# Linear attention followed by a mixture of adapters: the order of the second half rewritten, with the division moved to GpSimd for slots 18 to 35

## The chip, the cores and the metric

The kernel runs on one core of one Trainium2 chip. The core has TensorE (PE in the profile), VectorE (DVE), ScalarE (ACT), GpSimd (POOL) and SyncE (SP), which run side by side and wait for each other by semaphores; each takes its own instructions strictly in the order in which they were written. The metric is the device time of one execution in microseconds (us), and lower is better. A measurement of this kernel tells about 0.5% from no change.

## The reference

```
phi(x) = concat(relu(x) * cos(theta), relu(x) * sin(theta))      theta = pi/2 * position / S
kv  = sum over s of phi(k)[s,f] * v[s,d]      z = sum over s of phi(k)[s,f]
num = phi(q) @ kv                             den = phi(q) . z + 1e-6
x   = (num / den), heads side by side         q, k, v: 8 batches x 8 heads x 576 positions x 64
logits = x @ w_gate (8 experts); the two largest take part, weighted by their softmax
out = x + sum over the two experts e of weight_e * (x @ A[e]) @ B[e]          rank 16, float32 out
```

x has 4608 rows (batch and position) of 512 values.

## The kernel before

**Batches and slots.** Each of the 8 batches has a first part: q, k and v are loaded (float32 in memory, bfloat16 in the core's SBUF), v is multiplied by the cosine and by the sine of the position (`vs`: 9 position groups s, two tables i, so 18 instructions of 256 elements for each batch), k goes through relu (`rk`), and 72 small matmuls in three parts (`kv`) form the sums, which ACT copies to SBUF (`kve`). The 4608 rows of x are worked in 36 slots of 128 rows. Nine slots make two batches; the fifth of nine (4, 13, 22, 31) holds 64 rows of each of the two batches and is called mixed.

**The steps of a slot n.** `qc` relu of q, twice for a batch; `qt` four transposes on PE; `qe` DVE multiplies them by the tables into qT; `nd` PE forms numerators and denominators in one PSUM tile `nd` of 128 x 520 float32, of which there is only one; `re` DVE takes the reciprocals of the 8 denominators; `no` DVE multiplies the 512 numerators by them into x in bfloat16 (lines 354 to 363); `xt` PE transposes x; `xe` ACT copies that to SBUF; `za` PE forms gate logits and adapter products; for each group of three slots DVE finds the two largest logits and the weights (`mx`, `nm`, `mk`, `tt`, `cb`, `zg`, with a sigmoid `sg` on ACT), PE transposes (`zt`), and the result is copied (`ze`). `dx` is two matmuls of 512 columns that add x and the adapters' part in PSUM, `oe` copies the output row block to SBUF, `st` stores its 256 KB.

**nd in two forms.** Usually `nd` contracts 128 rows at once, with blocks of zeros in kv: 8 matmuls of 130 columns (line 343), 16 for a mixed slot. `by_rows(n)` chooses a form in which the two halves of the rows work side by side on 65 columns each, without the zeros: 16 matmuls at line 332. Before, that holds for slots from 27 on that aren't mixed.

**The order.** The text `ORDER` gives every step with its engine and arguments (`no,V,18` is step `no` of slot 18 on DVE; A is ACT, T PE, S SP, G GpSimd). Each engine's queue is the part of the text that names it, in that order; waits between engines follow from the data and the buffers. `W` is GpSimd too, with one wait more (lines 512 to 518): the instruction waits until the last `vs`, `rk` or `qc` of DVE ahead of it in the text is done. Loads are issued by GpSimd (line 215), stores by SP. `gate` (line 236) holds the stores back until the last v has arrived. The first 358 steps, up to `qc,V,4,1`, stay as they are.

Of the kernel before, what the change touches and what calls it, by code (L numbers as in the profile page):

```python
# [21 lines left out]
ldv,S,0,0 pre,G start,A ldk,S,0,0 ldw,S ldq,G,0,0 tq,A ldv,G,1,0 ldk,G,1,0 ldq,G,1,0 ldv,G,2,0 vs,A,0,3,0  # L22
vs,V,0,5,1 ldk,G,2,0 cols,V vs,A,0,4,1 vs,V,0,7,1 vs,A,0,5,0 kz,G,1 kz,V,2 vs,A,0,8,0 vs,A,0,8,1 vs,A,0,1,0
vs,V,0,4,0 vs,A,0,7,0 kz,V,0 vs,A,0,0,1 vs,A,0,2,1 vs,A,0,0,0 vs,V,0,6,0 vs,A,0,1,1 vs,A,0,3,1 rk,V,0,0 rk,A,0,1
vs,V,0,2,0 vs,V,0,6,1 kv,T,0,0 qc,V,0,1 kv,T,0,1 qc,V,0,0 kv,T,0,2 qt,T,1 kve,A,0,0 qt,T,0 kve,A,0,1 qe,V,0
cw,A,0 qe,V,1 dm,T,n0 dm,T,n0 dm,T,n0 nd,T,0 qt,T,3 re,V,0 qt,T,2 no,V,0 qe,V,3 vs,G,1,8,0 vs,A,1,3,1 dm,T,b0
dm,T,b0 nd,T,1 vs,A,1,5,0 vs,G,1,6,1 vs,V,1,2,0 xt,T,0 vs,A,1,6,0 vs,W,1,7,1 xe,A,0 re,V,1 qe,V,2 vs,G,1,5,1
vs,A,1,8,1 vs,G,1,0,1 no,V,1 vs,A,1,2,1 ldq,G,2,0 vs,A,1,4,1 vs,V,1,1,1 dm,T,b0 dm,T,b0 dm,T,b0 dm,T,b0 dm,T,b0
dm,T,b0 nd,T,2 vs,V,1,1,0 vs,A,1,0,0 rk,V,1,0 ldv,G,3,0 xt,T,1 vs,A,1,7,0 xe,A,1 vs,V,1,4,0 ldk,G,3,0 dm,T,b0
kv,T,1,0 vs,V,1,3,0 re,V,2 za,T,0 no,V,2 ldq,G,3,0 kv,T,1,1 mx,V,0 nd,T,3 qc,V,1,0 xt,T,2 kv,T,1,2 re,V,3  # L30
qc,V,1,1 xe,A,2 za,T,1 no,V,3 kve,A,1,1 qt,T,4 qt,T,5 kve,A,1,0 za,T,2 qe,V,4 xt,T,3 mx,V,1 xe,A,3 mx,V,2 nd,T,4
# [48 lines left out]
oe,A,28 zg,V,10 xt,T,34 nd,T,35 oe,A,27 st,S,26 xe,V,34 za,T,33 oe,A,29 re,V,35 zt,T,10 no,V,35 za,T,34 ze,A,10  # L80
st,S,29 mx,V,33 mx,V,34 xt,T,35 nm,V,11 st,S,28 dx,T,31,q1 mk,V,11 tt,V,11 dx,T,30,q0 cb,V,11 st,S,27 xe,V,35
sg,A,11 dx,T,32,b0 oe,A,31 zg,V,11 oe,V,30 za,T,35 oe,A,32 zt,T,11 st,S,31 mx,V,35 ze,A,11 mk,V,12 nm,V,12
zm,V,12 st,S,32 dx,T,33,b1 sg,A,12 dx,T,34,q1 zg,V,12 st,S,30 oe,A,33 zt,T,12 oe,V,34 ze,A,12 st,S,33 dx,T,35,q0
st,S,34 oe,A,35 st,S,35
# [20 lines left out]
def by_rows(n):  # L105

    return n >= ROWS and not mixed(n)


@with_exitstack  # L110
def kernel(ctx, tc, q, k, v, w_gate, A, Bw, out):
# [432 lines left out]
```

## Time and profile before

| what | value |
|---|---|
| median of 3 runs | 106.09 us (105.9 to 106.48) |
| profiled execution: its own time | 105.77 us |
| profiled execution: span of its instructions | 104.0 us |
| PE busy / weight loads | 91.5 us (88%) / 65.8 us (63%) |
| DVE busy | 86.7 us (83%), 264 instructions |
| ACT busy | 81.3 us (78%), 176 instructions |
| POOL busy | 57.6 us (55%), 112 instructions |

The span goes from the first to the last instruction; the profiled execution's own time is 1.8 us longer, and 0.3 us below the median. Busy time is what an engine spent in instructions; neighbouring instructions overlap by a few hundredths of a us, so that the distance from start to start is the better price of one. In the page's 40 slices, DVE and PE are in the highest tenth nearly throughout from the eleventh to the thirty-fourth; POOL is at zero from the thirtieth on.

### The profile page before, as it was taken

The numbers are of one execution on the slowest core, as the hardware profiler recorded it, in microseconds if no ns is written. First come the engines' busy times: TensorE is split into PE (matmuls) and PEld (weight loads), VectorE is DVE, ScalarE is ACT, GpSimd is POOL, SyncE is SP. The second block draws the span as 40 slices with busy tenths as digits, with TensorE's granted clock in tenths as the row PEclk, the third lists the DMA queues.
The fourth block names the chain that finished last, engine by engine and source line by source line (L and its number), as shares of the span: only waits on it lengthen the run. The fifth ranks groups of instructions, "written<-read, shape, count | busy, mean of one in ns | idle before, by whom it ended". The sixth has DMA issues, their size and how long they took to land.

```text
span 104.0 us, 3983 instructions
## 1 busy us (share of the span) xinstructions
PE 91.5 (88%) x1620; PEld 65.8 (63%) x1620; DVE 86.7 (83%) x264; ACT 81.3 (78%) x176; POOL 57.6 (55%) x112
## 2 busy tenths in 40 slices
PE   4999899779794999999999999999989899998710
PEld 1334467467573887867887788787778576665200
DVE  5058769579995999999999999999999899999700
ACT  6969757918898689999799969989975895966720
POOL 6991004960799696997979869999910000000000
PEclk9999999999999999999999999999999999999997
DMA  2999999999999999999999999999999985699993
GB/s 27 369 353 292 215 210 247 207 209 211 205 207 210 208 208 208 207 215 202 207 210 207 214 202 207 209 207 129 198 404 395 382 308 220 251 381 385 384 381 143
DMA packets 19225, 25.55 MB, mean 246 GB/s; under 512 B 2184, under 2 KB 13448, under 8 KB 19208
## 3 DMA queue, kind: packets, MB, share of 16 engines
q0 software_dynamic: 11616, 12.98, 73.8%
q1 hardware_dynamic: 7064, 12.21, 32.7%
q8 instruction: 12, 0.20, 0.7%
q10 hardware_dynamic: 528, 0.13, 0.6%
q14 instruction: 5, 0.04, 0.1%
HBM read 28.85 MB, written 9.44 MB: 368 GB/s over the span
## 4 chain that ended last, share of the span: by engine, by line
PE 40%; DMA 20%; DVE 12%; ACT 10%; POOL 9%; issue 2%; POOLq 0%; SPq 0%; ACTq 0%
DMA q<-in_q_dram 18%; PE nd L343 8%; PE big L275 6%; PE xz L368 5%; PE za L377 4%; PE out L459 4%; PE pq L308 4%; PE out L458 4%; POOL vs L259 4%; DVE xt L362 4%; DVE qT L316 3%; DMA out_dram<-v0f 3%; ACT kvsb L294 2%; DVE qq L301 2%; ACT vs L258 2%
## 5 line engine op out<-in xcount | busy, mean ns | idle before, releaser
L259 POOL TENSOR_SCALAR vs<-v,tab 128x256 bf16<-128x256 bf16 x78 | 38.2, 506 | 17.2 <-DMA v<-in_v_dram 8.7
L372 ACT COPY xT<-xz 128x512 bf16<-128x512 bf16 x34 | 19.9, 587 | 9.6 <-PE xz L368 9.2
L316 DVE TENSOR_TENSOR qT<-pq,tabq 128x1024 bf16<-128x1024 bf16 x36 | 23.9, 677 | 0.8 <-PE pq L308 0.8
L258 ACT ACTIVATE vs<-v,tab 128x256 bf16<-128x256 bf16 x43 | 20.1, 511 | 1.0 <-DMA v<-in_v_dram 0.7
L343 PE MATMUL nd<-kvsb,qT 128*128 128x130 bf16 (+1 forms) x256 | 19.1, 222 | 0.4 <-DVE qT L316 0.4
L362 DVE TENSOR_TENSOR xt<-nd,rden 128x512 bf16<-128x512 f32 x28 | 19.2, 686 | 0.3
L275 PE MATMUL big<-vs,k 64*64 64x130 bf16 x576 | 12.4, 221 | 3.5 <-DVE k L266 1.7
L343 PEld LDWEIGHTS <-qT 128*128 128x128 bf16 (+1 forms) x256 | 13.6, 100 | 2.9 <-issue 1.2
L368 PE MATMUL xz<-ident,xt 128*128 128x128 bf16 x144 | 14.1, 220 | 1.0 <-DVE xt L362 0.7
L377 PE MATMUL za<-AW,xT 128*128 128x136 bf16 x144 | 14.4, 223 | 0.0
L275 PEld LDWEIGHTS <-k 64*64 64x64 bf16 x576 | 9.1, 106 | 6.3 <-DVE k L266 2.5
L308 PE MATMUL pq<-ident,qq 128*128 128x128 bf16 x144 | 13.0, 219 | 0.0
L459 PE MATMUL out<-Ball,zgT 128*128 128x512 bf16 x31 | 11.8, 379 | 0.4 <-ACT zgT L440 0.4
L487 PE MATMUL nd<-ones 128*128 128x512 bf16 x36 | 10.6, 469 | 1.5 <-DVE eps_hi L488 1.5
L458 PE MATMUL out<-xt,turn 128*128 128x512 bf16 x31 | 11.7, 379 | 0.1
L368 PEld LDWEIGHTS <-xt 128*128 128x128 bf16 x144 | 10.1, 114 | 2.3 <-DVE xt L362 0.9
L294 ACT CAST kvsb<-big 64x520 bf16<-64x520 f32 x16 | 9.5, 595 | 1.5 <-PE big L275 1.3
L377 PEld LDWEIGHTS <-xT 128*128 128x128 bf16 x144 | 9.4, 98 | 1.9 <-ACT xT L372 0.8
L308 PEld LDWEIGHTS <-qq 128*128 128x128 bf16 x144 | 9.2, 98 | 1.8 <-DVE qq L301 0.2
L338 PE MATMUL nd<-eps_hi,ones 128*128 128x4 bf16 x56 | 9.5, 170 | 0.1
L487 PEld LDWEIGHTS <-ones 128*128 128x128 bf16 x36 | 4.1, 116 | 7.5 <-issue 3.6
L301 DVE TENSOR_SCALAR qq<-q 128x1152 bf16<-128x1152 bf16 x16 | 7.8, 491 | 0.8 <-DMA q<-in_q_dram 0.8
(81 smaller groups left out, 146.4 us busy)
## 6 DMA issues: line engine op xcount, KB each, us to landing
q<-in_q_dram POOLq DMA_DIRECT2D x8, 576.0 KB, 17.2
v<-in_v_dram POOLq DMA_DIRECT2D x7, 576.0 KB, 17.7
k<-in_k_dram POOLq DMA_DIRECT2D x7, 576.0 KB, 16.9
out_dram<-k SPq DMA_DIRECT2D x10, 256.0 KB, 3.6
out_dram<-v0f SPq DMA_DIRECT2D x8, 256.0 KB, 4.2
out_dram<-k0f SPq DMA_DIRECT2D x8, 256.0 KB, 3.3
out_dram<-v SPq DMA_DIRECT2D x6, 256.0 KB, 2.9
v0f<-in_v_dram SPq DMA_DIRECT2D x1, 1152.0 KB, 5.6
```

Of the source, the lines that this page charges most:

```text
L258: return e.activation(dst, src, AF.Copy, bias=0.0, scale=t)
L259: return e.tensor_scalar(out=dst, in0=src, scalar1=t, scalar2=1.0, op0=ALU.mult, op1=ALU.mult)
L275: e.matmul(out=big[halves[g2], par, gp * 2 * W:(gp + 1) * 2 * W], lhsT=k_b[b][pr, 2 * gp + g2, s, :], rhs=vs_t[b % NV][pr, s, 2 * gp + g2, ...
L308: e.transpose(out=d[:, gp, :, jj, :], in_=q2_t[b % 3][:, gp, s].rearrange("p g d -> p (g d)"), identity=ident)
L316: e.tensor_tensor(out=qT_t[n % NQ], in0=src, in1=tab, op=ALU.mult)
L343: e.matmul(out=nd[pr, par, gp * 2 * W:(gp + 1) * 2 * W], lhsT=qT[:, i, gp * 2 + par, js], rhs=kv_t[b % 3][:, par, gp, i, :], start=False, ...
L362: e.tensor_tensor(out=x.rearrange("p (a t d) -> p t a d", t=2, d=D), in0=nds()[:, :, :, 0:D], in1=rd.rearrange("p (t a) -> p t a", t=2).to ...
L368: e.transpose(out=xz[:, c * 128:(c + 1) * 128], in_=x[:, c], identity=ident)
L372: (e.copy if e is nc.scalar else e.tensor_copy)(xT_t[n % 3], src)
L377: e.matmul(out=zs[:, i, :], lhsT=xT_t[n % 3][:, c, :], rhs=AW[:, c, :], start=(c == 0 and i == 0), stop=(c == DCH - 1), skip_group_check=True)
L458: e.matmul(out=d, lhsT=turn, rhs=x_t[n % NX], start=True, stop=False)
L459: e.matmul(out=d, lhsT=zgT_t[g % 3][:, n - GROUPS[g][0], :], rhs=Ball, start=False, stop=True)
```

## The change

From the 359th step on the text of the order is a new one. In it, for slots 18 to 35 (`SPLIT`), ACT copies the 520 sums of `nd` to SBUF as float32 (`ev`), DVE takes the reciprocals from the copy, and GpSimd multiplies (`no` as G or W). Two buffers for the copies lie in the SBUF of k of batch 3. Of the 54 scalings of v for batches 5 to 7, DVE takes 14, ACT 12 and GpSimd 28 (before: none, 13 and 41). `xe` is on DVE 13 times (before 2), `ze` 4 times (0), `oe` 3 times (2), `kve` once (0); one `qc` goes to ACT. The loads of k and q of batch 7 come earlier in GpSimd's queue. The by-rows form now serves the slots 16, 18, 22, 27 and 29 to 35, the mixed ones 22 and 31 among them, where it takes 32 matmuls of 64 rows and 65 columns.

The number of every step but `ev` stays as it was.

```diff
-ROWS = 27
+ROWS = (16, 18, 22, 27, 29, 30, 31, 32, 33, 34, 35)
+SPLIT = (18, 19, 20, 21, 22, 23, 24, 25, 26, 27, 28, 29, 30, 31, 32, 33, 34, 35)
...
-    return n >= ROWS and not mixed(n)
+    return n in ROWS
...
+    nf_t = [k_b[3].rearrange("p g s d -> p (g s d)").bitcast(FP32)[:, i * 8 * W:(i + 1) * 8 * W]
+            .rearrange("p (t a x) -> p t a x", t=2, a=4) for i in range(2)]
...
+            parts = [(lo, tok[0][0]), (hi, tok[1][0])] if mixed(n) else [(slice(0, 128), tok[0][0])]
+            for js, b in parts:
+                for g2, pr in enumerate(halves):
+                    e.matmul(out=nd[js, g2, D:4 * W:W], lhsT=ones[pr, js], rhs=eps_hi2[pr], start=True,
+                             stop=False, skip_group_check=True)
...
+                        for js, b in parts:
+                            for g2, pr in enumerate(halves):
+                                e.matmul(out=nd[js, g2, a * W:(a + 1) * W], lhsT=qT[pr, i, a, js],
+                                         rhs=kv_t[b % 3][pr, par, gp, i, g2 * W:(g2 + 1) * W],
+                                         start=False, stop=(i == 1), skip_group_check=True)
...
+    def ev(e, n):
+        return e.copy(nf_t[n % 2].rearrange("p t a x -> p t (a x)"), nd[:, :, 0:4 * W])
+    def sums(n):
+        return nf_t[n % 2] if n in SPLIT else nds()
     def re(e, n):
-        e.reciprocal(rd_t[n % 2], nds()[:, :, :, D:W])
+        return e.reciprocal(rd_t[n % 2], sums(n)[:, :, :, D:W])
     def no(e, n):
...
+        return e.tensor_tensor(out=x.rearrange("p (a t d) -> p t a d", t=2, d=D), in0=sums(n)[:, :, :, 0:D],
+                               in1=rd.rearrange("p (t a) -> p t a", t=2).to_broadcast([128, 2, 4, D]), op=ALU.mult)
```

The queues that follow from the new text, as far as the prediction speaks of them, from the 359th step on:

```
GpSimd  vs,W,5,6,1 ldk,7 vs,W,5,7,1 vs,5,2,0 vs,5,2,1 vs,W,5,1,0 vs,W,5,5,0 vs,5,0,0 vs,W,5,4,0 vs,W,5,3,0 vs,W,5,5,1
        vs,5,6,0 ldq,7 no18 no,W,19 vs,5,3,1 no20 vs,W,6,6,1 vs,6,0,1 vs,6,5,0 no21 vs,6,7,0 vs,6,4,0 vs,6,2,0
        vs,6,7,1 no,W,22 vs,6,6,0 no23 no24 vs,7,4,0 vs,7,3,0 no,W,25 vs,7,6,1 vs,7,0,0 no26 vs,W,7,3,1 vs,7,5,1
        vs,7,7,0 vs,W,7,2,0 no27 no,W,28 no29 no,W,30 no,W,31 no,W,32 no33 no,W,34 no,W,35
PE, from kv of batch 7 to xt of slot 35
        kv,7,0 kv,7,1 za24 za25 kv,7,2 zt7 xt27 qt31 za26 nd30 qt32 xt28 dx21 nd31 qt33 xt29 dx22 qt34 nd32 xt30 zt8
        za27 za29 za28 nd33 xt31 dx23 qt35 nd34 xt32 dx24 za30 za31 za32 xt33 zt9 dx26 nd35 dx25 xt34 dx27 dx29 zt10
        za33 za34 dx28 xt35
```

## Rows read from the trace of the kernel before

**Rows 1.** Three windows: us, busy (instructions) of PE, PEld, DVE, ACT, POOL; clock, DMA share, GB/s

```profile
52.35:79.73 27.38, 27.01 (x568) 21.97 (x563) 27.05 (x81) 23.85 (x53) 21.71 (x43) 1.00 1.16 230
79.73:94.66 14.93, 14.17 (x264) 9.90 (x261) 13.99 (x48) 11.48 (x24) 0.00 (x0) 1.00 0.86 319
94.66:100.00 5.34, 3.90 (x23) 1.67 (x23) 3.65 (x15) 3.22 (x9) 0.00 (x0) 1.00 1.02 382
```

**Rows 2.** Timeline of PE: start, us, line, operation, out<-in, count, [idle before]

```profile
66.43 0.17 PE L338 MATMUL nd<-eps_hi,ones 128*128 128x4 bf16 x1
...
67.36 0.41 PE L368 MATMUL xz<-ident,xt 128*128 128x128 bf16 x4
...
74.30 0.38 PE L458 MATMUL out<-xt,turn 128*128 128x512 bf16 x1
...
74.73 0.38 PE L458 MATMUL out<-xt,turn 128*128 128x512 bf16 x1
...
75.16 0.17 PE L338 MATMUL nd<-eps_hi,ones 128*128 128x4 bf16 x1
...
75.68 0.38 PE L308 MATMUL pq<-ident,qq 128*128 128x128 bf16 x4
...
76.82 0.54 PE L275 MATMUL big<-vs,k 64*64 64x130 bf16 x24 [0.31 <-ACT u L421]
...
77.29 0.18 PE L325 MATMUL nd<-eps_hi,ones 64*128 64x4 bf16 x2
...
77.67 0.34 PE L434 MATMUL xz<-turn,zg 128*128 128x128 bf16 x3
77.85 0.40 PE L377 MATMUL za<-AW,xT 128*128 128x136 bf16 x4
78.08 0.39 PE L368 MATMUL xz<-ident,xt 128*128 128x128 bf16 x4
...
79.73 0.39 PE L368 MATMUL xz<-ident,xt 128*128 128x128 bf16 x4
...
94.72 0.38 PE L368 MATMUL xz<-ident,xt 128*128 128x128 bf16 x4 [0.33 <-ACT zgT L440]
```

**Rows 3.** Lines of 43 to 104 us: count, busy us, mean ns, idle before, releasers

```profile
L259 POOL TENSOR_SCALAR vs<-v,tab 128x256 bf16<-128x256 bf16 x53 | 25.8, 505 | 2.6 <-DVE qq L301 0.9 <-PE nd L343 0.8 <-DVE mk L399 0.7
...
L372 ACT COPY xT<-xz 128x512 bf16<-128x512 bf16 x24 | 14.1, 587 | 5.9 <-PE xz L368 5.6 <-PE xz L434 0.2
...
L362 DVE TENSOR_TENSOR xt<-nd,rden 128x512 bf16<-128x512 f32 x17 | 11.7, 686 | 0.2
...
L294 ACT CAST kvsb<-big 64x520 bf16<-64x520 f32 x10 | 6.0, 595 | 0.1
...
L301 DVE TENSOR_SCALAR qq<-q 128x1152 bf16<-128x1152 bf16 x9 | 4.6, 509 | 0.0
...
L266 DVE TENSOR_SCALAR k<-k 128x2304 bf16<-128x2304 bf16 x4 | 3.2, 812 | 0.0
...
L372 DVE COPY xT<-xz 128x512 bf16<-128x512 bf16 x2 | 0.8, 421 | 0.2 <-PE xz L368 0.2
```

**Rows 4.** Line L259, all of it: ns minimum/median/maximum, first and last start

```profile
L259 POOL TENSOR_SCALAR vs<-v,tab x78: 468/476/1068, 17.0 to 75.2; 128x256 bf16<-128x256 bf16 x78
...
L259 DVE TENSOR_SCALAR vs<-v,tab x5: 274/284/455, 17.4 to 21.5; 128x256 bf16<-128x256 bf16 x5
```

**Rows 5.** Timeline of POOL

```profile
52.70 5.48 POOL L259 TENSOR_SCALAR vs<-v,tab 128x256 bf16<-128x256 bf16 x12 [0.53 <-DVE qq L301]
...
59.01 0.79 POOL L215 DMA_DIRECT2D k<-in_k_dram  x1
...
72.81 1.07 POOL L259 TENSOR_SCALAR vs<-v,tab 128x256 bf16<-128x256 bf16 x1
```

**Rows 6.** Timeline of DVE, one instruction

```profile
72.73 0.81 DVE L266 TENSOR_SCALAR k<-k 128x2304 bf16<-128x2304 bf16 x1
```

**Rows 7.** Timeline of SP's queue, the stores

```profile
96.64 2.52 SPq L470 DMA_DIRECT2D out_dram<-k  x4
```

More of the change, by code (lines that the diff above doesn't have):

```diff
@@ L21 @@
 ORDER = """
[L22 to L31, printed above, removed]
@@ L82 @@
[L82 to L84 removed]
+ldv,S,0 pre,G start,A ldk,S,0 ldw,S ldq,G,0 tq,A ldv,G,1 ldk,G,1 ldq,G,1 ldv,G,2 vs,A,0,3,0 vs,V,0,5,1 ldk,G,2 cols,V
+vs,A,0,4,1 vs,V,0,7,1 vs,A,0,5,0 kz,G,1 kz,V,2 vs,A,0,8,0 vs,A,0,8,1 vs,A,0,1,0 vs,V,0,4,0 vs,A,0,7,0 kz,V,0
+vs,A,0,0,1 vs,A,0,2,1 vs,A,0,0,0 vs,V,0,6,0 vs,A,0,1,1 vs,A,0,3,1 rk,V,0,0 rk,A,0,1 vs,V,0,2,0 vs,V,0,6,1 kv,T,0,0
@@ new lines @@
+qc,V,0,1 kv,T,0,1 qc,V,0,0 kv,T,0,2 qt,T,1 kve,A,0,0 qt,T,0 kve,A,0,1 qe,V,0 cw,A,0 qe,V,1 dm,T,n0 dm,T,n0 dm,T,n0
+nd,T,0 qt,T,3 re,V,0 qt,T,2 no,V,0 qe,V,3 vs,G,1,8,0 vs,A,1,3,1 dm,T,b0 dm,T,b0 nd,T,1 vs,A,1,5,0 vs,G,1,6,1
+vs,V,1,2,0 xt,T,0 vs,A,1,6,0 vs,W,1,7,1 xe,A,0 re,V,1 qe,V,2 vs,G,1,5,1 vs,A,1,8,1 vs,G,1,0,1 no,V,1 vs,A,1,2,1
+ldq,G,2 vs,A,1,4,1 vs,V,1,1,1 dm,T,b0 dm,T,b0 dm,T,b0 dm,T,b0 dm,T,b0 dm,T,b0 nd,T,2 vs,V,1,1,0 vs,A,1,0,0 rk,V,1,0
+ldv,G,3 xt,T,1 vs,A,1,7,0 xe,A,1 vs,V,1,4,0 ldk,G,3 dm,T,b0 kv,T,1,0 vs,V,1,3,0 re,V,2 za,T,0 no,V,2 ldq,G,3 kv,T,1,1
@@ new lines @@
+rk,V,4,0 vs,W,4,2,1 oe,A,5 xt,T,12 mk,V,3 qt,T,16 re,V,13 tt,V,3 qt,T,15 vs,G,4,1,1 xe,A,12 no,V,13 dx,T,7,b1
+vs,G,4,7,0 vs,A,4,0,1 dx,T,8,b0 cb,V,3 qe,V,15 vs,G,4,5,1 sg,A,3 nd,T,14 oe,A,7 vs,G,4,4,0 zg,V,3 xt,T,13 oe,A,8
+vs,G,4,2,0 qt,T,17 re,V,14 zt,T,3 no,V,14 za,T,12 vs,A,4,6,0 vs,G,4,4,1 kv,T,4,0 xe,A,13 mx,V,12 vs,G,4,7,1 qe,V,16
+nd,T,15 vs,A,4,8,0 ldq,G,6 qc,V,4,0 xt,T,14 kv,T,4,1 re,V,15 qc,V,4,1 vs,W,5,6,1 kv,T,4,2 no,V,15 ldk,G,7 vs,W,5,7,1
+ze,A,3 xe,A,14 kve,A,4,1 gate,S,7 st,S,3 vs,G,5,2,0 vs,G,5,2,1 za,T,13 kve,A,4,0 qe,V,17 nd,T,16 re,V,16 mx,V,13
@@ L321, in nd_ @@
         if by_rows(n):
-            kvb = kv_t[tok[0][0] % 3]
-            for g2, pr in enumerate(halves):
-                e.matmul(out=nd[:, g2, D:4 * W:W], lhsT=ones[pr, 0:128], rhs=eps_hi2[pr], start=True,
-                         stop=False, skip_group_check=True)
+            parts = [(lo, tok[0][0]), (hi, tok[1][0])] if mixed(n) else [(slice(0, 128), tok[0][0])]
[3 more added lines that the diff above has]
+                             stop=False, skip_group_check=True)
             for gp in range(2):
@@ L329, in nd_ @@
                     for i in range(2):
-                        for g2, pr in enumerate(halves):
-                            a = gp * 2 + par
-                            e.matmul(out=nd[:, g2, a * W:(a + 1) * W], lhsT=qT[pr, i, a, :],
-                                     rhs=kvb[pr, par, gp, i, g2 * W:(g2 + 1) * W],
-                                     start=False, stop=(i == 1), skip_group_check=True)
+                        a = gp * 2 + par
+                        for js, b in parts:
[3 more added lines that the diff above has]
+                                         start=False, stop=(i == 1), skip_group_check=True)
             return
```

116 lines of the change are left out of this document (55 added, 61 removed).

## The prediction, on record before the run

> **What bounds the kernel now.** I read the windows first, because the change starts late: the 359th step falls at 52.35 us, and what matters are three stretches, each ending in a transpose that both orders have. In [rows 1] the reader is to see that from 52.35 to 79.73 us (the transpose of slot 27) PE is busy for 27.0 and DVE for 27.05 of 27.4 us, ACT for 23.9, and POOL for 21.7; that POOL is at zero from there on; that PE's clock is whole (1.00) in all three; and that the DMA engines are full while data still come in (share 1.16). From 79.73 to 94.72 (the transpose of slot 35) PE has 14.2 and DVE 14.0 of 15 us. The rest is the tail of the last slot. So two engines are full and one has nothing to do at the end.
>
> Busy PE is not yet PE at its peak, so I priced its steps from start to start in the timeline [rows 2]: a normal nd 0.52 us (75.16 to 75.68), a mixed one 0.93 (66.43 to 67.36), one by rows 0.38 (77.29 to 77.67), a third of kv 0.47 (76.82 to 77.29), zt 0.18, and za, xt and qt 0.23 each (77.85 to 78.08); a dx 0.43 (74.30 to 74.73). With the counts of the old text PE's work from 52.35 to 79.73 is 12 dx, 9 kv, 10 normal nd, one mixed, two by rows, 39 of 0.23 and 4 zt: 26.0 of 27.4 us. From 79.73 to 94.72 it is 9 dx, 1 kv, 6 nd by rows, 1 mixed, 21 of 0.23, 3 zt: 3.87 + 0.47 + 2.28 + 0.93 + 4.83 + 0.54 = 12.9 of 15.0, so 2.1 us are gaps. PE bounds the first stretch; the second is PE plus gaps, in which PE waits for one slot's nd to be read before it writes the next (there is one nd tile).
>
> **The change, part by part.** *PE.* Up to the transpose of slot 27 the new text has one third of kv and one nd by rows more, one za less, and slots 16 and 18 (0.14 each) and 22 cheaper: +0.47 + 0.38 - 0.23 - 0.28 - 0.18 = +0.2. A mixed nd by rows isn't in the trace: 32 small matmuls at the pace of kv's 24 in 0.47 give 0.63 and the epsilon ones 0.08 more, two row forms would be 0.76; I take 0.75. PE alone would thus reach slot 27's transpose when it did.
>
> *DVE*, with [rows 3, 4]. To that point it loses 10 normalisations (0.686, so 6.9) and 2 qc (1.0) and gains 14 scalings (0.284, so 4.0), 6 xe (0.421, so 2.5) and three passes over PSUM (one kve, one oe, one qe; at most 0.69 each, 2.1): +0.7. After it, it loses 8 normalisations and a qe (6.2) and gains 5 xe, 3 ze (at most 0.42), a qc and an oe (4.6): -1.6. DVE would be at slot 27's xe at about 80.4, and has slack from there.
>
> *ACT.* The copy `ev` isn't in the trace; the nearest row is kve, 520 float32 values from PSUM in 0.595 us [rows 3], and a narrower or a wider one can hardly be far from it (xe 0.587). 12 of them to slot 27 are 7.1; six xe, one kve and one oe go (4.7), a scaling and a ze go (1.0), one qc comes (between one xe and 2.25 of them by its size, 0.59 to 1.3; I take 1.1). Net +2.5 on 23.9 of 27.4 us [rows 1]. It fits with 1 us to spare; ACT hides the copies, but its cover is thin, and a copy that comes late holds back both the next nd and the division.
>
> *GpSimd* is where the sum is made. Its queue is in order, and the last scaling of batch 7 that kv,7,0 needs (position group 2) stands behind nine normalisations; behind that come slot 27's normalisation and the rest. From its start at 52.70 [rows 5]: 28 scalings at 0.46 (12 in 5.48), 12.9; two load issues at 0.79, 1.6; nine normalisations at X; and what DVE takes of the port.
>
> X isn't in the trace. GpSimd's scaling of 256 elements takes 0.476 [rows 4]. The least is one such, 0.48; twice the elements is 0.95; if the second operand cost as much again it would be 1.9. I take 0.95, the nearest row by elements, and keep 0.48 to 1.9 for the range. The Trainium skill speaks against that, GPSIMD Engine Reference, § 3.1 "Elementwise — side-by-side cycle accounting": two inputs share one read port, about 2.6 cycles an element at 1.2 GHz, so an estimate of 1.11 us for 512; no run here shows it, and the time by it is with the rivals.
>
> The port: a DVE pass over SBUF with one tensor and a GpSimd scaling get in each other's way. The scaling that began at 72.81 took 1.07 instead of 0.476 while DVE's relu of k (72.73, 0.81 long) ran [rows 5, 6]. Over 43 to 104 us, 53 scalings averaged 505 instead of 476, 1.5 us in all, and POOL idled 0.9 + 0.7 us for DVE's relus; DVE did 4.6 + 3.2 us of them [rows 3]. So 3.1 over 7.8: 0.40 us lost for each us of DVE. Ahead of that scaling the new text has DVE do 13 scalings, 3 qc and 3 rk, 3.7 + 1.5 + 2.4 = 7.6 us, so 3.0 us (nothing if all fall beside load issues, 7.6 if none overlaps). The Trainium skill, SBUF — State Buffer, § "Who interferes with whom", has the second comer block fully; the 72.81 row lost 0.59 of 0.81, so the trace lies between.
>
> Sum: 52.7 + 12.9 + 1.6 + 9 x 0.95 + 3.0 = 78.7. kv of batch 7 then starts at 78.8, and PE's work from it to slot 35's transpose is 3 kv, 11 za, 4 zt, 8 xt, 5 qt, 5 nd by rows, the mixed one and 9 dx: 1.41 + 2.53 + 0.72 + 1.84 + 1.15 + 1.90 + 0.75 + 3.87 = 14.2. For the gaps I take 1.1, about half of the 2.1 before: nd is free after one copy of 0.6 instead of a reciprocal and a pass of 0.69, but four engines now take turns instead of two (0 to 2.1). That ends at 94.07 instead of 94.72: **0.65 us sooner**.
>
> *The tail.* Slot 35 needs a copy (0.6), a reciprocal and GpSimd's pass (0.95) between nd and xt; PE has 4 dx, xt, zt and 2 za to do there, 2.6 us, which hides them; without that cover it would be 0.9 later. After xt of slot 35 both texts have six dx and the same chain. Stores: four take 2.52 us [rows 7], 0.63 each; from slot 23's on 14 are left, 8.8 us, while PE from dx of slot 23 to the last has 13 dx, 11 of 0.23, two nd and 4 zt, 9.6 us and its gaps. So the store queue isn't late. The earlier loads of k and q of batch 7 cost 1.6 us of GpSimd as before, and can't land much sooner behind full DMA engines; nothing waits for them.
>
> The profiled execution took 105.77 us; 0.65 less is 105.1. The median of the runs is 0.32 above it, so **105.4**.
>
> **The rivals.**
> GpSimd late (the other side): with its queue behind, kv of batch 7 waits, PE can't pass it, and all after it moves by the same amount. It decides from 0.65 us on, at X = 1.02, or at a port loss of 0.49 instead of 0.40. At X = 1.15 it is 1.8 us later, 106.09 + 1.15 = 107.2. For it: POOL goes from 21.7 busy us of 27.4 to 26 and more with its waits, in a stretch where three others are full too. Against: eight normalisations come after that stretch, where POOL was idle.
> By the GPSIMD Engine Reference's estimate of 1.11 us this rival gives 106.9.
> Port locked whole, as a mechanism of its own: each us of DVE's 7.6 is lost, 4.6 more than reckoned, 110.0. The 72.81 row lost 73%, the average over the stretch was 40%, so 0.05 at most; it is the rule of SBUF — State Buffer that the trace bears out only in part.
> No change: the gaps stay at 2.1 since each slot now passes four engines, 94.07 + 1.0, so 106.4. For it: PE's gaps after 79.73 came from other engines' turns as well as from nd.
> More gain: X near 0.8 or a port loss half as large; then kv of batch 7 waits for PE itself, which has 24.1 us of work and 1.4 of gaps ahead of it, 77.9 instead of 78.8; 104.5.
>
> **How the numbers follow.** The forecast 0.40 (0.27 of it clear of the 0.5%, 0.13 within), more gain 0.14, no change 0.13, GpSimd late with the locked port 0.33. Half a per cent, 0.53 us, is about what can be told from no change. So faster 0.41, the same 0.26, slower 0.33. The forecast's own range is 104.8 to 106.1; eight in ten reaches from the greater gain to GpSimd late with X about 1.2, 103.9 to 107.8.
>
> **What would show it.** In the profile after, GpSimd's normalisation and its mean give X at once. kv of batch 7 should start near 78.8 and be released by a GpSimd scaling; if it starts at 80 or later the sum's first half is wrong. From it to slot 35's transpose there should be about 15.3 us. ACT's copy should be 0.6. If PE waits mainly for ACT between 52 and 79 us, or SP's queue is unbroken over the last 10 us, the cause lies in neither of my two places.

## The result and the profile after

The kernel after the change takes **107.59 us** (median of 6 runs, 107.15 to 108.0), the kernel before, run beside it, 106.0 us (105.56 to 106.57): a ratio of 1.0145, with 95% interval 1.0104 to 1.0185. It is slower by 1.6 us; the forecast was 105.4, faster by 0.65. Every median here counts all executions of a kernel, while the ratios leave out those in which the chip was in a slower state, so that a ratio can differ from the quotient of two medians. The profiled execution took 107.65 us, its span is 105.9 us.

Three windows of the kernel after, ending in the same transposes as [rows 1] (slot 27, slot 35) and with the tail; the columns are those of [rows 1].

```profile
52.35:83.74 31.39, 28.40 (x622) 22.26 (x616) 30.74 (x93) 26.32 (x57) 25.77 (x40) 1.00 1.11 245
83.74:96.14 12.40, 12.05 (x242) 9.19 (x242) 11.36 (x48) 9.91 (x21) 8.26 (x8) 1.00 0.80 298
96.14:105.90 9.76, 4.01 (x23) 1.62 (x22) 3.10 (x14) 3.83 (x9) 0.00 (x0) 0.94 0.73 271
```

The reader is to see three things. Slot 27's transpose comes at 83.74 instead of 79.73, 4.0 us late. The stretch from it to slot 35's takes 12.40 us instead of 15.0 and gives 2.6 of them back; most of these are less PE time in that stretch (12.05 against 14.17: the new text has a third of kv and one nd less there, and slot 31 in the cheaper form), the rest smaller gaps. And in the first stretch DVE is busy for 30.74 of 31.39 us, while PE has 3.0 us of gaps; before, both were full [rows 1]. The tail is 0.5 us longer (9.76 against 104.0 - 94.72 = 9.28).

Where DVE's time went, by line, engine and operation, from 52.35 to 83.74 us in the kernel after (count, busy us, mean ns, idle before). These are the rows that answer to [rows 3].

```profile
L259 DVE TENSOR_SCALAR vs<-v,tab 128x256 bf16<-128x256 bf16 x14 | 6.2, 473 | 0.0
L301 DVE TENSOR_SCALAR qq<-q 128x1152 bf16<-128x1152 bf16 x6 | 3.6, 603 | 0.0
L266 DVE TENSOR_SCALAR k<-k 128x2304 bf16<-128x2304 bf16 x3 | 3.2, 1065 | 0.0
...
L259 POOL TENSOR_SCALAR vs<-v,tab 128x256 bf16<-128x256 bf16 x28 | 13.6, 500 | 1.4 <-DVE k L266 0.8 <-PE big L275 0.5
L368 POOL TENSOR_TENSOR xt<-k,rden 128x512 bf16<-128x512 f32 x7 | 7.4, 1058 | 2.6 <-DVE rden L359 2.1 <-DVE za L420 0.6
L364 POOL TENSOR_TENSOR xt<-k,rden 128x512 bf16<-128x512 f32 x3 | 3.5, 1169 | 0.9 <-DVE m L389 0.9
```

DVE's scaling, 284 ns in the median of the five before [rows 4], averages 473; its relu of q 603 (509 before) and of k 1065 (812 before) [rows 3]. That is 14 x 0.189 + 6 x 0.094 + 3 x 0.253 = 2.65 + 0.56 + 0.76 = **4.0 us longer than the same passes at those prices**. DVE's passes that read PSUM keep theirs: the copies `xe` take 412 ns in the mean of 6 in this stretch (421 in [rows 3]). GpSimd's division X is 1.04 us undisturbed. The timelines show how the passes meet; first GpSimd's rows, then DVE's, of the kernel after (start, us, line, operation, [idle before]).

```profile
59.31 1.43 POOL L364 TENSOR_TENSOR xt<-k,rden 128x512 bf16<-128x512 f32 x1
...
71.65 1.05 POOL L368 TENSOR_TENSOR xt<-k,rden 128x512 bf16<-128x512 f32 x1
73.20 1.15 POOL L368 TENSOR_TENSOR xt<-k,rden 128x512 bf16<-128x512 f32 x1 [0.51 <-DVE rden L359]
...
76.28 1.04 POOL L368 TENSOR_TENSOR xt<-k,rden 128x512 bf16<-128x512 f32 x1 [0.94 <-DVE rden L359]
...
78.20 1.04 POOL L368 TENSOR_TENSOR xt<-k,rden 128x512 bf16<-128x512 f32 x1
80.03 1.84 POOL L259 TENSOR_SCALAR vs<-v,tab 128x256 bf16<-128x256 bf16 x4 [0.79 <-DVE k L266]
```

```profile
59.77 1.06 DVE L259 TENSOR_SCALAR vs<-v,tab 128x256 bf16<-128x256 bf16 x1
...
71.87 1.14 DVE L301 TENSOR_SCALAR qq<-q 128x1152 bf16<-128x1152 bf16 x1
72.94 0.19 DVE L359 RECIPROCAL rden<-k 128x8 f32<-128x8 f32 x1
73.05 0.41 DVE L301 TENSOR_SCALAR qq<-q 128x1152 bf16<-128x1152 bf16 x1
73.38 1.26 DVE L259 TENSOR_SCALAR vs<-v,tab 128x256 bf16<-128x256 bf16 x2
...
78.40 1.46 DVE L266 TENSOR_SCALAR k<-k 128x2304 bf16<-128x2304 bf16 x1
```

The relu of q that begins at 71.87, while GpSimd divides from 71.65 to 72.70, takes 1.14 us; the next one, begun at 73.05 ahead of GpSimd's next division, 0.41. The relu of k that begins at 78.40 inside the division of 78.20 to 79.24 takes 1.46 (0.81 in [rows 6]), and the scaling of 59.77, inside the division that ends at 60.74, 1.06 instead of 0.284. So these three grew by 0.73, 0.65 and 0.78 us, where 0.83, 0.84 and 0.97 us of the division were left: each waits out nearly all that is left of GpSimd's pass, all but 0.1 to 0.2 us, and then does its own work. It works the other way as well: the division that begins at 73.20, inside the relu of 73.05, takes 1.15 instead of 1.04. GpSimd also waits for DVE in order: 0.94 for the reciprocal at 76.28, 0.79 for the relu at 80.03 (this one is an order's wait, a W).

The kernel before had shown the same, at a smaller price since GpSimd's passes were short there. A relu of q (first DVE's row, then GpSimd's scaling beside it) took 0.79 instead of 0.41:

```profile
57.71 0.79 DVE L301 TENSOR_SCALAR qq<-q 128x1152 bf16<-128x1152 bf16 x1
...
57.71 0.47 POOL L259 TENSOR_SCALAR vs<-v,tab 128x256 bf16<-128x256 bf16 x1
```

Three rows of PE fix the places of the sum:

```profile
66.05 0.20 PE L325 MATMUL nd<-eps_hi,ones 64*64 64x4 bf16 x4
...
81.43 1.15 PE L275 MATMUL big<-vs,k 64*64 64x130 bf16 x48
...
83.74 0.39 PE L374 MATMUL xz<-ident,xt 128*128 128x128 bf16 x4
```

The sums of batch 7 start at 81.43, where the prediction has 78.8. GpSimd isn't what they wait for: PE is busy with slot 29's nd right up to them. Only their last third finds GpSimd's last scaling just done (it ends at 81.87), which costs them 0.2 us at most. The chain of work that ended last runs through DVE (start, us, engine, line):

```profile
78.48 1.38 DVE k L266
79.86 0.33 DVE xT L378
...
80.42 0.61 DVE qT L316
...
81.08 0.42 PE nd L333 x16
81.50 0.39 PE big L275 x16
```

In this chain every longer piece from 52.5 to 81.1 us is one of DVE, but for PE from 62.3 to 65.5, and none is GpSimd's. Of PE's gaps to transpose 27 the waits that the profile names come to 2.3 us: 1.8 for DVE's qT and relus of q (0.6, 0.5, 0.4, 0.3), 0.5 for GpSimd's divisions.

### The profile page after: what moved, and what is told of

It is laid out like the page before. It is cut to its first block, busy times and chain, and to the rows that moved or that the text cites. A ratio compares the mean times of both kernels' runs of the same rounds, so it can differ in the third digit from the quotient of the medians.

```text
span 105.9 us, 4091 instructions
## 1 busy us (share of the span) xinstructions
PE 89.9 (85%) x1650; PEld 65.4 (62%) x1664; DVE 87.5 (83%) x276; ACT 82.9 (78%) x177; POOL 70.9 (67%) x117
## 4 chain that ended last, share of the span: by engine, by line
DVE 35%; PE 26%; DMA 17%; POOL 9%; ACT 4%; issue 3%; POOLq 0%; DVEq 0%
DMA q<-in_q_dram 17%; DVE qT L316 8%; DVE vs L259 5%; PE za L383 4%; DVE qq L301 4%; POOL vs L259 4%; PE big L275 4%; PE xz L374 4%; DVE k L266 3%; DVE xt L368 3%; PE nd L344 3%; PE pq L308 3%; PE out L464 2%; DVE rden L359 2%; DVE xT L378 2%
## 5 line engine op out<-in xcount | busy, mean ns | idle before, releaser
L259 POOL TENSOR_SCALAR vs<-v,tab 128x256 bf16<-128x256 bf16 x65 | 32.5, 513 | 15.8 <-DMA v<-in_v_dram 8.4
L344 PE MATMUL nd<-kvsb,qT 128*128 128x130 bf16 (+1 forms) x216 | 16.8, 221 | 1.1 <-DVE qT L316 1.0
L378 ACT COPY xT<-xz 128x512 bf16<-128x512 bf16 x23 | 13.5, 589 | 4.5 <-PE xz L374 4.2
L344 PEld LDWEIGHTS <-qT 128*128 128x128 bf16 (+1 forms) x216 | 12.0, 99 | 3.7 <-DVE qT L316 1.8
L364 POOL TENSOR_TENSOR xt<-k,rden 128x512 bf16<-128x512 f32 x10 | 10.8, 1081 | 4.5 <-DVE rden L359 1.7
L353 ACT COPY k<-nd 128x520 f32<-128x520 f32 x18 | 10.8, 601 | 3.2 <-PE nd L333 1.2
L383 PE MATMUL za<-AW,xT 128*128 128x136 bf16 x144 | 13.0, 223 | 0.2
L368 DVE TENSOR_TENSOR xt<-nd,rden 128x512 bf16<-128x512 f32 x17 | 11.7, 686 | 0.2
L493 PE MATMUL nd<-ones 128*128 128x512 bf16 x36 | 10.0, 448 | 1.5 <-DVE eps_hi L494 1.5
L464 PE MATMUL out<-xt,turn 128*128 128x512 bf16 x29 | 11.0, 380 | 0.2
L368 POOL TENSOR_TENSOR xt<-k,rden 128x512 bf16<-128x512 f32 x8 | 8.4, 1056 | 3.7 <-DVE rden L359 2.1
```

Of the source, the lines that this page charges most:

```text
L259: return e.tensor_scalar(out=dst, in0=src, scalar1=t, scalar2=1.0, op0=ALU.mult, op1=ALU.mult)
L344: e.matmul(out=nd[pr, par, gp * 2 * W:(gp + 1) * 2 * W], lhsT=qT[:, i, gp * 2 + par, js], rhs=kv_t[b % 3][:, par, gp, i, :], start=False, ...
L368: return e.tensor_tensor(out=x.rearrange("p (a t d) -> p t a d", t=2, d=D), in0=sums(n)[:, :, :, 0:D], in1=rd.rearrange("p (t a) -> p t a" ...
L378: (e.copy if e is nc.scalar else e.tensor_copy)(xT_t[n % 3], src)
L383: e.matmul(out=zs[:, i, :], lhsT=xT_t[n % 3][:, c, :], rhs=AW[:, c, :], start=(c == 0 and i == 0), stop=(c == DCH - 1), skip_group_check=True)
L464: e.matmul(out=d, lhsT=turn, rhs=x_t[n % NX], start=True, stop=False)
```

## The experiments

All times are medians beside the kernel before, which stood at 106.0 to 106.16 us in these runs. "Transpose 27" is xt of slot 27 in the profile: 79.73 before, 83.74 after.

**e1: the division in two halves** (cut: `o`, `i0` and `i1` are the output and the two inputs of the division).

```diff
...
+        if n in SPLIT and e is nc.gpsimd:
+            done = [e.tensor_tensor(out=o[:, t], in0=i0[:, t], in1=i1[:, t], op=ALU.mult) for t in range(2)]
+            return done[0]
+        return e.tensor_tensor(out=o, in0=i0, in1=i1, op=ALU.mult)
```

> The changed kernel, with each of GpSimd's 18 normalisations issued as two of 256 values instead of one of 512 (1.06 us). Theory 1 (collisions: DVE's passes over SBUF stand behind a whole GpSimd pass, so the long passes delay DVE, which sets the pace up to slot 27): the longest wait halves, DVE's 14 scalings fall from a mean of 473 ns to about 380 and its reluctant relus of k from 986 to about 850, and the time falls by about 0.8 us, to 106.8. Theory 2 (queue: GpSimd itself is late because its passes are long): 18 more instructions at about 0.1 us each, 9 of them before the last scaling of batch 7, so about 0.9 us more, 108.5.

Measured: 108.03 us (107.77 to 108.22), ratio to before 1.0206 [1.018, 1.0232], 0.4 above the changed kernel; transpose 27 at 83.84. Rows of the stretch up to there:

```profile
L259 DVE TENSOR_SCALAR vs<-v,tab 128x256 bf16<-128x256 bf16 x14 | 5.6, 428 | 0.0
L301 DVE TENSOR_SCALAR qq<-q 128x1152 bf16<-128x1152 bf16 x6 | 4.3, 723 | 0.0
L266 DVE TENSOR_SCALAR k<-k 128x2304 bf16<-128x2304 bf16 x3 | 3.3, 1110 | 0.0
...
L372 POOL TENSOR_TENSOR xt<-k,rden 128x256 bf16<-128x256 f32 x20 | 13.1, 677 | 2.5 <-DVE rden L359 1.3 <-DVE m L394 0.9 <-DVE za L425 0.3
```

Two halves cost 2 x 0.677 = 1.35 us in the mean instead of 1.09, 0.26 for the further instruction where theory 2 had 0.1, and DVE's three kinds take 13.2 us instead of 13.0: shorter pieces back to back free nothing.

**e2: the new row form in the old order** (kernel before, `ROWS` as after, no copies).

```diff
-SPLIT = (18, 19, 20, 21, 22, 23, 24, 25, 26, 27, 28, 29, 30, 31, 32, 33, 34, 35)
+SPLIT = ()
```

> The kernel before with its own order and engines, and only the larger set of slots whose nd goes by rows (16, 18, 22, 27, 29 to 35). PE saves 0.14 us each for slots 16 and 18, and about 0.5 each for the mixed 22 and 31 (0.41 measured in the changed kernel, 0.93 before), 1.3 in all. If PE bounds both stretches: 0.8 us less than before, 105.2. If DVE is as full as PE (theory: either engine alone gives nothing): 0.3 less at most, 105.7, and PE's gaps grow by about what nd saves.

Measured: 106.84 us (106.03 to 107.42), ratio 1.0073 [1.0042, 1.0104]. Both expectations (105.2 and 105.7) are missed: the row halves by themselves don't help, they lose. In the profile DVE waited 0.9 us for k of batch 7 to land; why it came late isn't explained here.

**e3: DVE's 14 scalings of batches 5 to 7 as a memset** (that part of the sums is left out).

```diff
+        if e is nc.vector and b >= 5:
+            return e.memset(dst, 0.01)
```

> The changed kernel with DVE's 14 scalings of v for batches 5 to 7 replaced by a memset of the same 256 elements (so these parts of the sums are left out), which should take about as long by itself (0.27 us) but reads nothing from SBUF. Theory 1 (collisions): the 14 take about 0.28 instead of 0.473 us, GpSimd's passes beside them are shorter too, and the time falls by 2 to 2.5 us, to about 105.3. Theory 2 (GpSimd's queue): DVE's delay doesn't decide, at most 0.4 us less, 107.2. If the memset collides just as the scaling does, nothing changes and the run tells the two apart no further.

Measured: 106.96 us (106.7 to 107.13), ratio 1.0097 [1.007, 1.0124], 0.6 below the changed kernel; transpose 27 at 82.97.

```profile
L303 DVE TENSOR_SCALAR qq<-q 128x1152 bf16<-128x1152 bf16 x6 | 4.1, 684 | 0.0
L260 DVE MEMSET vs<- 128x256 bf16 x14 | 3.8, 272 | 0.1
L268 DVE TENSOR_SCALAR k<-k 128x2304 bf16<-128x2304 bf16 x3 | 3.7, 1244 | 0.0
```

The memset isn't lengthened (272 ns each of the 14 times, beside a GpSimd busy 25.5 of 30.6 us), and 2.4 us go from these 14. But the relus behind them now take the wait: 684 and 1244 instead of 603 and 1065. Only 1.4 us leave the three kinds together. By its time this run spoke for theory 2, GpSimd's queue; but its rows show that much of the wait had only moved to the next pass that needs the port. It decides nothing by itself.

**e4: the division on GpSimd late only, in the old order** (e2's row form; division of slots 27 to 33, with the copies put in and `xe` of slots 28 to 33 on DVE; one of the seven places is shown).

```diff
-nd,T,29 qe,V,30 st,S,4 kve,A,7,1 xt,T,28 tt,V,8 st,S,9 re,V,29 qt,T,32 cb,V,8 no,V,29
+nd,T,29 ev,A,29 qe,V,30 st,S,4 kve,A,7,1 xt,T,28 tt,V,8 st,S,9 re,V,29 qt,T,32 cb,V,8 no,G,29
```

> The kernel before with its own order up to slot 26 and the new set of row halves; the copy by ACT and the normalisation by GpSimd only for slots 27 to 33, when no scaling of v is left on GpSimd, and the xe of slots 28 to 33 on DVE. Theory 1 and 2 agree that it is faster than the changed kernel, since there is neither a collision nor a queue: about 105.0 to 105.5. Theory 3 (four engines in turn lose more than the moved work gives): not better than the row halves alone, and PE's gaps after slot 27's transpose stay at 2 us or more.

Measured: 109.4 us (109.26 to 109.99), ratio 1.034 [1.0305, 1.0375]. From transpose 27 to 35 it takes 16.0 us instead of 15.0. DVE's waits in its last stretch (waited for, us in total, times, longest):

```profile
DVE rden L359 <- ACT k L353: 4.0, 6, 1.5
```

The reciprocal stands where it stood, right behind nd; now a copy lies between, and DVE's whole queue waits for it. In this order the late division loses; e8, e11 and e12 give it the order of the changed kernel.

**e5: the division of slots 18 to 27 over one head of eight** (64 of 512 values; the rest of x is left out there; queue and waits stay).

```diff
...
+            if 18 <= n <= 27:
+                o, i0, i1 = o[:, 0, 0:1], i0[:, 0, 0:1], i1[:, 0, 0:1]
```

> The changed kernel, but GpSimd's division of slots 18 to 27 multiplies only one of the eight heads (64 of 512 values; the other values of x in these slots are left out). The queue and every wait stay. Ten passes of 1.06 us shrink to at most the 0.47 of a scaling, so at least 5.9 us leave GpSimd's queue up to slot 27, nine of them (5.3 us) ahead of batch 7's last scaling, and DVE's two-port passes meet less of them. Theory A, GpSimd's queue bounds the stretch: the sums of batch 7 start when PE gets there, slot 27's transpose comes back from 83.7 to 80.0 to 80.7 us, the time from 107.6 to 104.0 to 104.8. Theory B, DVE held up at the port bounds it: only what DVE lost to the long passes comes back, about half of 4.5 us at most and with scalings still colliding: transpose 27 at 82 to 82.5, time 105.8 to 106.5. Theory C, the order with four engines in turn is the cost: 107.0 or more.

Measured: **105.18 us** (104.2 to 106.28), ratio 0.9896 [0.9852, 0.9939]; transpose 27 at 80.48. By line from 43 to 104 us, and then the windows up to transpose 27 and on to transpose 35:

```profile
L259 DVE TENSOR_SCALAR vs<-v,tab 128x256 bf16<-128x256 bf16 x14 | 4.0, 312 | 0.0
L301 DVE TENSOR_SCALAR qq<-q 128x1152 bf16<-128x1152 bf16 x8 | 3.8, 471 | 0.0
L376 POOL TENSOR_TENSOR xt<-k,rden 128x64 bf16<-128x64 f32 x10 | 3.4, 342 | 6.6 <-DVE rden L359 3.1 <-DVE m L396 2.3 <-DVE za L427 1.2
```

```profile
52.35:80.48 28.13, 27.55 (x642) 22.16 (x633) 27.04 (x93) 26.02 (x57) 18.35 (x40) 1.00 1.16 244
80.48:92.89 12.41, 12.41 (x245) 9.21 (x243) 11.27 (x48) 10.01 (x21) 8.31 (x8) 1.00 0.97 356
```

All but 0.75 us of the 4.0 come back at transpose 27, as theory A (GpSimd's queue) had put it; the time, 105.18, misses that theory's 104.0 to 104.8. But DVE's passes are short again too: the same relu of k took 0.74 here and 1.46 there. The edit took away both suspects at once, so it named the division and not the way in which it costs. The tail took 0.65 of the gain (103.3 - 92.89 = 10.4 us). The DMA engines, 0.80 busy in the stretch ahead of it after the change, are 0.97 busy there in this run, which may be why; no run tests it.

**e6: e5 and e3 together** (both parts are left out).

> As the kernel with short divisions in slots 18 to 27, and DVE's 14 scalings of batches 5 to 7 replaced by a memset of the same 256 elements as well (both parts of the result are left out). Memset alone gave 0.6 us back. Theory A: nothing more than with the short divisions alone (within 0.3 us), 104.0 to 104.8. Theory B: the two together free DVE, 1 us or more below the short divisions alone, 104.5 to 105.5. Theory C: 106.5 or more, since neither part was what cost.

Measured: 105.56 us (104.94 to 106.57), ratio 0.9955 [0.9916, 0.9993]; transpose 27 at 80.54, in e5 80.48. Nothing on top of e5 (the time is even 0.4 higher): without the long divisions there is nothing to win by taking the scalings off the port.

**e7: the changed kernel with the old row form.**

```diff
-ROWS = (16, 18, 22, 27, 29, 30, 31, 32, 33, 34, 35)
+ROWS = tuple(n for n in range(27, 36) if n != 31)
```

> The changed kernel with the row form of nd as before: slots 27 to 35 but for 31, so 16, 18, 22 and 31 in the old form again and 28 in the new. PE loses 0.14 + 0.14 + 0.5 + 0.5 and wins 0.14. If PE bounds neither stretch, 107.4 to 107.9, the same; if PE bounds the stretch up to slot 27, +0.8; if it bounds only the one behind, +0.3 to +0.5, 108.0.

Measured: 107.63 us (107.53 to 107.75), ratio 1.0149 [1.0111, 1.0187], what the change has. The row halves are worth nothing in the time. Up to transpose 27 (83.93, 0.2 later) PE doesn't bound. Behind it PE does:

```profile
83.93:96.75 12.82, 12.82 (x226) 9.54 (x224) 11.49 (x48) 10.12 (x21) 8.30 (x8) 1.00 0.78 286
```

PE has no gap there, and the stretch is 0.42 us longer than 12.40, near the 0.5 that slot 31's nd costs more in the old form. The tail is shorter by as much as both delays (9.15 us instead of 9.76), for a reason that isn't shown.

**e9: 11 of GpSimd's scalings left out** (that part of the sums is missing), divisions whole. This run and e10 separate what e5 had left together: GpSimd's queue is shorter by as much as in e5, but DVE still meets the long passes.

```diff
 (steps taken out of the text of the order)
-vs,G,5,2,0 vs,G,5,2,1 vs,G,5,0,0 vs,G,6,0,1 vs,G,6,5,0 vs,G,6,7,0
-vs,G,6,4,0 vs,G,6,2,0 vs,G,7,4,0 vs,G,7,3,0 vs,G,7,6,1
```

> The changed kernel with 11 of GpSimd's 28 scalings of v for batches 5 to 7 left out (that part of the sums is left out), none of those that wait for DVE; its divisions stay whole. That takes 11 x 0.47 = 5.2 us out of GpSimd's queue, as much as the short divisions took, but leaves the 1.04 us passes behind which most of DVE's lengthened passes stood. If the length of GpSimd's queue is what came back with the short divisions: transpose 27 at 80.5 to 81.2 instead of 83.7, time 105.2 to 105.8. If it is DVE held up at the port behind the long passes: DVE's scalings still average over 400 ns, transpose 27 at 82.7 or later, time 106.6 to 107.4.

Measured: **106.95 us** (106.33 to 107.51), ratio 1.0088 [1.0046, 1.0129]; transpose 27 at 83.19. Up to there:

```profile
L258 DVE TENSOR_SCALAR vs<-v,tab 128x256 bf16<-128x256 bf16 x14 | 5.9, 448 | 0.0
...
L265 DVE TENSOR_SCALAR k<-k 128x2304 bf16<-128x2304 bf16 x3 | 2.9, 956 | 0.0
...
L363 POOL TENSOR_TENSOR xt<-k,rden 128x512 bf16<-128x512 f32 x3 | 3.6, 1196 | 4.2 <-DVE m L388 4.2
```

5.2 us less in GpSimd's queue move transpose 27 by 0.55. GpSimd spends them idle: before these three divisions alone it stands 4.2 us for DVE (0.9 in the changed kernel). DVE's passes are nearly as long as in the changed kernel (448 and 956 instead of 473 and 1065). Theory A falls.

**e10: every DVE pass that could meet GpSimd a memset of its undisturbed length** (scalings, relus of k and q from batch 5 on; these parts are left out), GpSimd's queue whole.

```diff
 (in the relu of k, and the same in that of q; the scaling as in e3)
...
+        if b >= 5:
+            return e.memset(dst[:, :, 0:3], 0.5)
         return e.tensor_scalar(out=dst, in0=src, scalar1=0.0, scalar2=None, op0=ALU.max)
```

> The changed kernel, GpSimd's queue whole, but from batch 5 on every pass of DVE that could meet GpSimd at the port becomes a memset of about its undisturbed length: the 14 scalings (256 elements), the relus of k (768 of 2304) and of q (384 of 1152); these parts of the computation are left out. If DVE held up at the port is the cause, it wins back its 4 to 5 us, transpose 27 at 80.3 to 81.2, time 105.0 to 105.8, and GpSimd waits less for DVE. If the length of GpSimd's queue is the cause, only what the memset of the scalings gave and a little more: transpose 27 at 82.2 to 83, time 106.3 to 107.

Measured: **105.47 us** (104.2 to 106.65), ratio 0.9927 [0.9877, 0.9976]; transpose 27 at 80.44. Up to there:

```profile
L261 POOL TENSOR_SCALAR vs<-v,tab 128x256 bf16<-128x256 bf16 x28 | 12.9, 474 | 0.8 <-DVE qq L307 0.5 <-DVE k L269 0.2
L374 POOL TENSOR_TENSOR xt<-k,rden 128x512 bf16<-128x512 f32 x7 | 7.3, 1043 | 1.1 <-DVE za L426 0.6 <-DVE rden L365 0.5
```

```profile
52.35:80.44 28.09, 27.55 (x629) 22.07 (x619) 26.76 (x92) 26.03 (x57) 24.52 (x40) 1.00 1.17 249
```

All of GpSimd's work is there, 24.5 of 28.1 us, and 3.3 of the 4.0 us are back. The memsets also do less than the passes they stand for (about 0.7 us less: 3.8 + 2.1 + 1.9 against 14 x 0.284 + 3 x 0.81 + 5 x 0.41), so that up to 0.7 of the 3.3 can be that. PE is busy 27.55 us of 28.1 in this run and in e5: it is the bound again in both. This run frees both engines of each other; that it is DVE's side of the wait that cost is what e9 says, where GpSimd had time to spare and nothing came of it, and the chain above. So the cause is DVE held up at the port behind GpSimd's divisions.

**e8, e11, e12: the second half alone.** The kernel before up to a seam, then the steps that are left in the order of the changed kernel; nothing of the division is on GpSimd while batches 5 to 7 are scaled. e8 has the seam at nd of slot 27. e11 has it at nd of slot 28; e12 at 27; both have slot 29's nd behind the transpose of slot 27, and e12 slot 28's behind the second part of batch 7's sums.

```diff
 (kernel before up to zg,V,7)
-nd,T,27 st,S,3 qc,V,7,1 zt,T,7 st,S,20 re,V,27 za,T,24 no,V,27 xt,T,26
+st,S,3 st,S,11 st,S,14 nd,T,27 ev,A,27 re,V,27 qe,V,29 no,G,27 nd,T,28 xt,T,26 ev,A,28 nd,T,29
 (e8; from here in the changed order)
```

> The kernel before up to nd of slot 27, step for step; from there on the steps that are left in the order of the changed kernel, with copies by ACT and division by GpSimd for slots 27 to 35, and the row form for 27 and 29 to 35. It has no scaling of v on DVE for batches 5 to 7 and no division on GpSimd while GpSimd still scales v. If the gain behind slot 27 (12.4 us to slot 35's transpose instead of 15.0) is the second half's own: transpose 27 at 79.7 to 80.5, transpose 35 at 92.5 to 93.2, time 104.0 to 104.8, which beats both kernels. If it is only a backlog made up (DVE, ACT and the stores come to slot 27 with less behind them because they had waited before), then 105.5 to 106.5. If GpSimd's turn in each slot is a loss by itself, as in the run with the division moved in the old order, 107 or more.

Measured: e8 **105.17 us** (104.93 to 106.15), ratio 0.9937 [0.9894, 0.9979]. The window from transpose 27 to 35, and two rows of DVE at the seam:

```profile
81.96:94.36 12.40, 12.40 (x245) 9.20 (x242) 11.27 (x48) 9.95 (x21) 8.28 (x8) 1.00 0.92 341
```

```profile
78.50 0.20 DVE L359 RECIPROCAL rden<-k 128x8 f32<-128x8 f32 x1 [1.04 <-ACT k L353]
...
81.41 0.17 DVE L389 MAX8 m<-za 128x8 f32<-128x8 f32 x1 [1.18 <-PE za L383]
```

From transpose 27 to 35 it takes 12.40 us again, with PE unbroken. But transpose 27 came at 81.96, 2.2 us later than before, so that transpose 35 is only 0.36 sooner; DVE lost 1.04 and 1.18 us at the seam, where it stood for the first copy and for PE behind that. The time falls between the two cases expected, so this run alone doesn't say how much of the gain is the second half's own.

> The spliced kernel with its seam moved: the kernel before up to nd of slot 28, then the changed order for slots 28 to 35, with nd, copy and reciprocal of slot 29 put behind the transpose of slot 27. At the first seam DVE stood 1.0 and 1.2 us and PE 0.7 and 0.5 us waiting for the first copies, and slot 27's transpose came at 82.0. If that is the seam's own cost: transpose 27 at 79.7 to 80.3, transpose 35 some 12.5 to 13.3 us later, time 103.2 to 104.0. If the first seam's late start only moved gaps that the second half would have had anyway: transpose 35 at 94 or later, time 105 to 105.6.

> The spliced kernel with its seam at nd of slot 27 as at first, but nd of slots 28 and 29 put behind the second part of batch 7's sums and behind the transpose of slot 27, so that PE doesn't wait for the first copies, and DVE's qT of slot 29 ahead of slot 27's reciprocal. If the waits at the seam were the cost: transpose 27 at 80 to 80.8, time 103.5 to 104.3; if GpSimd's division of slot 27 itself (a copy, a reciprocal and 1.04 us in a chain instead of a reciprocal and 0.69 us) is: transpose 27 at 81 or later, time 104.6 or more, above the seam at slot 28.

Measured: e11 **104.89 us** (104.64 to 105.17), ratio 0.991 [0.9881, 0.9939]; e12 105.49 us (104.57 to 107.05), 0.9912 [0.987, 0.9954]. Both mend the seam as the better case had it (transpose 27 at 80.11 and 80.32), and both miss that case's time, since transpose 35 comes at 94.04 and 94.08. In e11:

```profile
80.11:94.04 13.93, 13.60 (x266) 9.76 (x260) 11.78 (x50) 10.56 (x23) 8.30 (x8) 1.00 0.92 343
```

PE does 13.6 us there instead of 12.4, since with this seam more of its work stands behind transpose 27; of the 1.85 us won at transpose 27 only 0.3 are left at transpose 35 (94.36 to 94.04). e12 shows the port once more, with one division moved ahead of a relu of q (first a row of GpSimd, then one of DVE):

```profile
78.78 1.04 POOL L364 TENSOR_TENSOR xt<-k,rden 128x512 bf16<-128x512 f32 x1 [2.99 <-DVE rden L359]
```

```profile
79.17 0.96 DVE L301 TENSOR_SCALAR qq<-q 128x1152 bf16<-128x1152 bf16 x1
```

All three are below the kernel before, by 0.6 to 0.9%, with intervals clear of no change, and e11 by 1.1 us: with the division on GpSimd only once its scalings of v are over, the second half of the change pays. Of e11's gain 0.7 us is there at transpose 35 (94.04 against 94.72), the rest is a shorter tail. How much is the division's and how much that of the new order and of `xe` on DVE isn't shown; e4 shows that the division without that order loses.

## Why the prediction was wrong, by its steps

*PE* held and didn't matter up to slot 27. It has 3.0 us of gaps in the first stretch, and a mixed nd by rows took 0.41 us (66.05 to 66.46), not 0.75. The row halves that I counted as 0.46 us of gain there are worth nothing in the time (e7).

*DVE* is the step that failed: "+0.7 [...] and has slack from there". Its busy time to transpose 27 rose by 30.74 - 27.05 = 3.7 us. The lengthening by the port alone is 4.0; without it the +0.7 would have been -0.3. I priced the 14 scalings at 0.284, the median of five [rows 4], though one of these five, begun beside a GpSimd scaling, took 0.455 (the maximum there), and took the port's price from a row where GpSimd was the one that waited [rows 5, 6]. So the sum charged 3.0 us to GpSimd and nothing to DVE. It is paid by whoever comes second, and with passes of 1.04 us on GpSimd it is mostly DVE, a full engine. The row at 57.71 in the kernel before has DVE paying 0.38 us, and I didn't look for it.

The rate of 0.40 was no price of the port either. Of its 3.1 us over 7.8 only 1.5 are scalings made longer, 0.19 for each us of DVE; the other 1.6 is idle time in which GpSimd waits in order for a step of DVE (for the 0.7 [rows 3] name `mk`, not a relu). And a rate for each us of DVE can't carry over from GpSimd passes of 0.47 us to those of 1.04, when what a pass loses is what is left of the other engine's pass.

The Trainium skill, SBUF — State Buffer, § "Who interferes with whom", says just this of DVE instructions in a 2-port mode: the engine that issues first has the pair of ports that both share for its whole instruction, and the other is blocked entirely. The rows at 71.87 and 78.40 agree, but for the last 0.1 to 0.2 us of the other's pass. I had taken it up as a rival for GpSimd alone, and gave it 0.05 because the row at 72.81 lost 73%. That was read wrongly: 0.59 is 73% of the whole relu, but of that relu only 72.81 to 73.54 was left, and 0.59 of 0.73 us is all but 0.14, as near to the rule as the rows after.

*GpSimd*: X is 1.04 undisturbed where I took 0.95. Its last scaling for batch 7's first sums ended at 81.87, where the sum has 78.7: from 52.7 on it was busy for 24.8 us where I had 23.05 (12.9 + 1.6 + 8.55), and stood idle for 4.3 (0.65, 0.55, 0.88, 0.51, 0.94, 0.79 in its timeline) where I had 3.0 for the port. Both together are 3.1 more. But all of that idle time is waiting for DVE, and e9 shows that a shorter queue only waits longer. The prediction had the sums released by a GpSimd scaling; they started at 81.43 behind PE's own work, which was late by its waits for DVE. The Trainium skill's GPSIMD Engine Reference, § 3.1 "Elementwise — side-by-side cycle accounting", led to an estimate of 1.11 us; the measured 1.04 lies nearer to it than to mine.

*ACT*: the copy took 0.601 us in the mean of 18 (I had 0.6), and hid.

*From kv of batch 7 to transpose 35*: 14.7 us (81.43 to 96.14) where I had 15.3. Of the 0.6 less, 0.34 is the mixed nd at 0.41 instead of 0.75; the gaps, reckoned as in the prediction, are 0.85 where I had 1.1. In the stretch behind transpose 27 PE is busy for 12.05 of 12.40 (in e5 and e8, with the same order there, for all of it).

*The tail*: 0.5 us longer where I had no change. SP's stores are unbroken from 95.58 to 102.03 us (before, from 94.03 to 100.51), with two pauses of 0.9 and 0.5 us just ahead of that. Why the tail is longer is left open.

*The rivals*: "GpSimd late" gave 107.2, near to what came, and its condition X > 1.02 was met. Its mechanism, PE waiting for GpSimd's queue, isn't what happened: that the number came near is luck. "No change" and "more gain" fell; e5 and e10, in both of which batch 7's sums start at 78.4 behind a full PE, show what "more gain" meant.

## What to carry to other kernels

Before moving work to GpSimd, list DVE's passes over SBUF in the same stretch: each of the kinds seen here (one bf16 tensor read from SBUF and written there) waits out most of what is left of the GpSimd pass that it meets, and the longer that pass, the longer the wait; the price goes to whichever engine comes second, so look in the trace for rows in which either one pays, and charge it to both. Put such work where the other engine has few of these passes left: with divisions on GpSimd only late, and the order of the new second half, 1.6 us of loss became 1.1 us of gain. When a run removes a suspect, see whether its wait has moved to the next instruction (e3), or whether the edit took two suspects at once (e5), before it decides anything.

## What the runs showed of the hardware that I had not expected

A DVE memset of 256 values takes 272 ns beside GpSimd's long divisions (e3) and beside the short ones (e6) alike; a scaling of the same size takes 473 beside the long ones and 312 beside the short. A GpSimd product of two tensors takes 1.04 us for 512 values and 0.29 for 64 where nothing disturbs it. The by-rows form costs hardly more for a mixed slot (0.41 us for slot 22 in the kernel after) than for another (0.38 for slot 27 in the kernel before), though it has twice the matmuls.
